# One order of 679 tasks for another in a sparse-attention and maxout kernel

## The chip, the cores and the metric

The kernel runs on one NeuronCore of a Trainium2 chip. The core has a matmul engine (PE; PEld is its weight load), three engines for elementwise work (DVE, ACT, POOL), and SP, which in this kernel does nothing but issue DMAs. Each engine works through its own list of instructions in order; semaphores make one wait for another. The metric is the device time of one execution, in microseconds, lower being better.

## The reference

Four batches, eight heads, 768 positions, head size 64. Each query sees the keys less than 16 positions away and, besides, 24 block summaries (the maximum of the keys and the mean of the values over blocks of 32). The result goes through a maxout layer.

```python
k_sum = k.reshape(B, H, nb, block, D).max(axis=3)
v_sum = v.reshape(B, H, nb, block, D).mean(axis=3)
scores_l = scale * q @ k.T        # kept where |i - j| < 16
scores_s = scale * q @ k_sum.T + log(32)
a = softmax(concat([scores_l, scores_s]))
x = a @ concat([v, v_sum])        # heads side by side: 3072 x 512
out = maximum(x @ w1, x @ w2) @ w_out
```

The kernel uses max(h1, h2) = h1 + relu(h2 - h1): it forms wd = w2 - w1, computes relu(x wd) w_out, and adds x (w1 w_out), with the product w1 w_out (called w1o) made once on the chip.

## The kernel before

The program is a list of 679 tasks. Each is made by `op` (L112) with the engines that may do it, a planned duration for each, what it reads and writes, and a label. `Plan.run` (L128) emits them in the sequence of the string `ORDER` (L20): each word has a letter for the engine (P, A, D, G for POOL, S for SP), the task's number, and the buffer slots that it takes. So `ORDER` fixes three things: the engine of each task, the sequence on each engine, and the slots. The planned durations are not read by `Plan.run`; of a table such as `{"SP": 1.3, "DVE": 1.0}` it looks only at which engines are named.

A task must wait for the tasks whose results it reads, for the former users of its slot, and for all that stands before it on its engine. The slots are few: 8 PSUM banks (most PE tasks take one or two), 8 landing buffers for loads (`land`), 4 for cast keys and queries (`kqb`), 1 for cast values (`vb`), 2 for spread values (`vx`), 4 for outputs (`o`).

The stages, with their lines, for batch b and head pair p:

- **Loads** (SP): keys and queries of a head pair, 384 KB each (`load_kq`, L305); values of half a batch, 768 KB (`load_v`, L327); the weights w1 and w2 in halves of 1 MB each (`load_w12`, L599) and w_out in two halves (`load_wo`, L629).
- **Keys and queries**: a cast to bf16 (L419), transposes on PE ("turn k", "turn q", L434), a copy out of PSUM ("place k", "place q", L453 and L465), for keys also the block maximum ("max", L454), a wrapped copy ("wrap", L458) and the summaries set into place ("sums", L461).
- **Values**: a cast (L331), five copies that spread them over tiles ("spread v", L371 to L377 and L387 to L393), block means on PE ("means", L346 or L349), their copies, and one copy that repeats them over all tiles ("spread means", L379 and L395). In batch 0 they are done in two halves of four heads. DVE, POOL, ACT (batch 0) or a DMA issued by SP can do a spread.
- **Attention**: "scores" (PE, L501), "exp" (ACT, L515), in batches 1 to 3 "mask" (DVE, L509), "values" (PE, L543), "inv" and "x" (DVE, L549 and L552), "turn x" (PE, L575) and its copy "xt". A score or value task carries two pairs of digits, head pair and group of 256 positions: "scores 0 01 11" is batch 0, pairs 0 and 1, group 1.
- **Weights**: "wd" (DVE or POOL, L607), "w1b" (cast, L610), "turn w1" (PE, L618), "w1t" (copy), "wo" (cast, L633), "w1o" (PE, L644: two half sums per quarter).
- **Maxout**, for each batch and group: four "hidden" tasks (PE, L660, eight matmuls of 256 columns), four "relu" (L666), then for each 128 rows "out" (PE): four matmuls with w1o (L674), twice four with w_out (L681), a copy (L685) and a store (SP, L692).

PE is used in four shapes: 128 rows by 128 columns (hidden, out, w1o, means of batch 0), 64 by 128 (all turns and the scores), 128 by 64 (values) and 128 by 32 (later means).

In the order before, the first loads are k02, k03, q02, k00, k01, q01, q00, v00, q03, v01, then the weights w1, w2 (first halves), w1 (second half), w_out (both halves), w2 (second half). The names k02 and so on are batch and head pair.

Of the kernel before, what the change touches and what calls it, by code (L numbers as in the profile page):

```python
# [17 lines left out]


ORDER = (  # L20
    "D3 S38:0,0 D6:0 S40:1,0 D1 D0 G7 D2 G4:0 S39:0 S12:2,0 S36:3,0 S37:0 G8 A92:0 S13:0 G5:0 A101:1 "
    "S14:4 P103:0,0 A93:2 P94:2,0 D105:3,0 G23:0,0,0 G9 A96:1,0 G32:0,0 S41:0 D68:3 D11:0 P70:4,0 S16:5 "
    "D97:0 P95:0 A77:1 D72:0,0 S42:6 P79:6,0 G78:0 D73:1 A81:2,0 G10 P80:0 D75 A100:0 D82:1 G69:3 D74 "
    "P71:0 D85:1 A76:2 S43:7 D83 D84 P88:2 D106:1 S52:0 P90:6 A89:0 D15:0,0 P86:4 A91:1 D19 P24:2 D102:2 "
    "D98 P104:0 D18 A25 S62:3 A20 D26 D22 A87:2 D17:0 S65:2 D108 A31 P33:3 D107 D21 A109:3 D27 D99 A34 "
    "D28 P114:6 A45:0 D29 P110:4 S53:4 D30 A115:3 P112:0 D35 P46:2 A111:4 G49:1 P116:6 D47:1,0 D117:0 "
    "A113:5 G48:0 S146:1,0 D118:0,0 P121:2 P126:4 D122:1 P50:6 D123:1,0 P119:0 D51:0 P124:2 A59:0 G44:0 "
    "D120:0 P131:6 S147:0 D125 A55:1 P60:0 D127:2 D128:0 P460:2 G63:0 A64:0 P56:3 D461:0 P458:5 S152:5,0 "
    "D57:0 A61:0 P455:2 D132:0 D133:0 P449:3 G66:0 A67:0 P136:0 P446:4 S150:6,0 D137:1 D138:0 P456 S153:0 "
    "P134:6 P450 D58:0 A135:1 S151:0 A457:0 P447 D54:0 S156:7 A451:0 P452:0 A448:0 S154:3 D218:1 P139:6 "  # L30
    "A219:0 P129:1 P453 D130 G257:3 A459 S149:2,0 D140:2 P220:3,0 P221:0 A454:0 G163:1,0,0,0 P480:1 "
    "D222:0,0 S148:0 A226:1 P141:6 P462:2 A481:1 D142:2 D223:1 A258:2 P482:5 G246:1 D143:0 A463 P464:0 "
    "D225 D224 D245:0 P144:3 S177:0,0 P227:6 A465 P476:1 D145 A228:2 D483 P484:2 A477 G157:0,0 P247:3,0 "
    "P248:0 P260:5,0 P259:0 D253:2 P471:0 A261:2,0 S172:4,0 D249:1,0 P478:7 A265:0 P472 D262:0 A479 "
    "P500:1 G155:0 D250:1 P489:3 A501:2 D229 A231:0 S161 P473 D263 S160 D264 G230:1 P164:4 S173:0 A474:0 "
    "P485 D168 S162 A165 D252 D159 P232:5,0 P266:0 P233:0 A234:3,0 P490 D166 D158 A167 P486 A238:3 S169 "
    "D235:0 S170:1,0 P491 A267:4 S171:0 D236 D237 P494:7 S180:5 D492:1 A487:2 P239:4 D251 S178:6 D495 "
    "P242:0 P269:2 A240:0 P496:6 D268 S174:7,0 A243:5 P498:7 D241 S475 P507:4 A497 D499 G294:2 A270:1 "
    "P272:0 P284:5 P502:7 D273:0 D244 A307:3 D271 P254:2 P503 A255:3 D274:2,0 S175:0 P508 D285:1 A295:1 "
    "D286:0,0 P275:0 D256 P287:2 P278:5 P509 G181:0,0 D288:2 D279:0 D289:0 P504 A510:3 D276:1 D280:0 "  # L40
    "S194:3,0 G306:0 P466:2 D277:0 P281:3 S488 P297:5,0 D282:2 P290:0 S176:0 A302:1 D283:0 P296:0 G179:0 "
    "P467 D291:3 A298:0,0 S493 P292:3 P468 G321:1 A505:0 D293 S186:0,0,0 G184 P188:5 D299:1 P309:0,0 "
    "S198:2,0 P308:0 P323:6,0 A314:3 P534:3 D310:3,0 S506 A469:2 P512:4 S182 D535:1 A325:2,0 S185 P518:0 "
    "D311:0 G187:0 G322:2 S470 P514:1 D333:3 A519:2 S196:1,0 D313 A513 P516:2 D312 D327 D326:0 G334:0 "
    "A515 P532:3 A517 G370:1 D189 D190 P335:0,0 S197:0 P336:0 D328 P324:0 A337:1,0 D533 P520:4 S183 "
    "A341:0 P530:2 D338:0 S199:0 A329:2 P521 D191 D339 S195:0 D300 A531 D340 P315:0 D192 P330:6 D193 "
    "P345:2 A316:2 P525:5 S204:5 A331:4 P522 D317 P536:0 A346:0 S200:4,0 D301 P543:1 D537 S202:6 P342:6 "
    "D332 P318:2 P544 A343:1 D347 S201:0 P552:0 A319:5 P303:6 D553:0 P545 G371:3 A304:3 P548:2 D320 "
    "A523:1 D344 S511 P526 A549 G382:0 D546:0 P354:6 P357:3 G397:2 P351:0 D355:0 P550:2 D356:1,0 D358:1 "
    "P527 D352:2 A551 D359:2,0 P554:6 D353:0 D305 P538:7 A555 A528:2 P373:2,0 P372:0 G383:3 P384:0,0 "  # L50
    "D378:2 P561:4 A374:2,0 G205:0,0 P348:5 A386:1,0 D375:0 P360:2 P562 D349:0 G203:0 P539 D350:0 D361:1 "
    "P563 D362:0 G410:1 S206:1,0,0 P363:5 A564:3 S529 P556:2 G409:0 D364:2 D365:0 S565 P366:3 D387:1 S208 "
    "P385:0 P368:5 A367:0 G398:3 P540 D369 G211:0 P557 A390:0 D377 D541:2 P570:3 D376 S542 D388 P558 D389 "
    "D571:2 P608:4 D209 A559:3 P411:5,0 S560 P394:0 D609:1 P379:2 P412:0 A395:5 S210 P579:7 D413:3,0 "
    "P572:4 A380:4 D417:3 P568:0 D207 A573 P400:5,0 P399:0 D414:0 P391:1 P590:3 A392:2 D401:0,0 P566:4 "
    "D416 D569 P588:1 A567 D403 D415 A591:0 P574:2 D393 A589 D402:1 P212:0 A405:1 P575 D213 A214 D215 "
    "P584:4 D381 D404 P576 D216 A585 D217 P406:5 P421:0 P580 A407:3 P592:3 D577:2 A422:1 P418:4 S578 P581 "
    "A419:0 D423 P586:6 D582:3 P604:2 S583 D587 S547 P602:0 D420 A605 D408 P593 A603 P439:4 P433:6 P424:1 "
    "P594 D425:0 D440:1 D441:0,0 P597:0 A595:2 D426:1,0 P606:4 S596 D434:2 D396 P598 A607 D435:0 P427:1 "
    "P436:3 P430:5 D428:1 P610:7 D437:0 D438:0 P599 D429:0 D431:2 P611 A600:3 D432:0 P615:3 S601 P442:1 "  # L60
    "P444:4 A443:3 P612 D445 P616 D613:0 P620:0 P674:6 P644:4 P660:5 D645:2 P658:1 P626:2 P622:7 A627:0 "
    "A621 P624:4 D623 P633:2 P642:0 P638:7 D643 P617 A639 A625 P646:0 D618:2 A661:1 P651:7 P634 P656:4 "
    "P640:3 A657 P664:5 D641 P662:4 P635 D663 P652 D659 A636:3 P647 S637 S619 P628:3 S524 P665 S614 "
    "P669:4 P629 P653 P666 A654:3 P630 S655 A667:2 P648 S668 D631:1 P675 S632 D649:0 P670 P676 S650 P671 "
    "A677:3 D672:2 S678 S673 "
)


# [34 lines left out]
class Plan:  # L103
# [8 lines left out]
    def op(self, engine, us, fn, read=(), write=(), change=(), touch=(), behind=(), prio=0.0, label="",  # L112
           port=False, lanes=(0, 1)):
        t = Task()
        t.port, t.lanes = port, lanes
        t.engine, t.us, t.fn, t.label = engine, us, fn, label
        t.on = us if isinstance(us, dict) else {engine: us}
        t.prio = (prio, len(self.tasks))
        t.new, t.behind = [*write, *change], behind
        t.deps = {w for b in (*read, *change) for w in b.writers}  # L120
        for b in t.new:
            b.writers.append(t)
        for b in (*read, *touch, *t.new):
            b.users.append(t)
        self.tasks.append(t)
        return t
# [20 lines left out]
def kernel(  # L147
# [15 lines left out]
    B, H, S, D = 4, 8, 768, 64  # L163
# [10 lines left out]
    op = plan.op  # L174
# [123 lines left out]
    def load_kq(b, hp, prio):  # L298
        f = Buf(land)
        for n, src in enumerate((k, q)):  # L300
            part = Buf(Ring([None]))
            view = lambda f=f, n=n: f.ap[:, 768 * n:768 * n + 768].rearrange("p (h c) -> p h c", h=2)
            kqin[b, hp, n] = f, part, view
            op("SP", {(0, 0, 0): 1.5, (0, 0, 1): 1.6, (0, 1, 0): 1.75}.get((b, hp, n), 1.09),
               lambda view=view, src=src: nc.sync.dma_start(  # L305
                out=view(), in_=src[b, 2 * hp:2 * hp + 2].rearrange("h (p j) d -> p h (j d)", j=J)),
               write=[f, part], prio=prio, label=f"load {'kq'[n]}{b}{hp}")

    v_spread, vx_part = {-1: []}, {}
# [73 lines left out]
    def later_values(b, prio):  # L383
        vb, parts = load_v(b, prio, 0, {"POOL": 1.52})
        kw = dict(write=[vx[b], *vx_part[b]], prio=prio + 2)
        last = []
        for piece, (lo, hi, tiles_, part, ms) in enumerate(PIECES):  # L387
            share = (1, 1, 1, 5 / 6, 1 / 6)[piece]
            last.append(copy({"SP": 0.05 + 2.15 * share * (hi - lo) / 64, "DVE": 0.1 + 0.87 * share,
                              "POOL": 0.1 + 2.9 * share},  # L390
                             lambda lo=lo, hi=hi, tiles_=tiles_, part=part, ms=ms: (
                                 rows(vx[b].ap[lo:hi, tiles_]), rows(vb.ap[part:part + hi - lo, ms])),
                             read=[vb], label=f"spread v{b}{piece}", **kw))  # L393
        mean = means(b, vb, [vb], 0, H, vx_part[b], prio + 2)
        v_spread[b] = [*last, copy({"SP": 2.1, "DVE": 1.9, "POOL": 5.7}, lambda: mean_rows(b, 0, H),  # L395
                                   read=[mean], label=f"spread means {b}", **kw)]

    def copy(us, aps, label, relu=False, **kw):
# [383 lines left out]
```

The softmax here doesn't subtract the row's maximum and nothing guards it: scores larger than these inputs give would overflow.

## Time and profile before

| | us |
|---|---|
| runs | 173.26, 173.74, 174.13, 174.36 (median 173.94) |
| the execution that was profiled | 174.36 |
| its span in the profile | 172.7 |
| PE busy | 154.5 |
| DVE busy | 113.4 |
| ACT busy | 89.2 |
| POOL busy | 40.3 |

The span begins 1.66 us short of the whole time of that execution. The granted clock of PE was 1.00 in every stretch. A row of the chain of waits gives a start, a length, and the engine and line that the end depended on; in a timeline, x is a count of instructions, and the bracket tells how long the engine stood idle before them and what released it. The duration of one instruction in a merged row is not the row's length divided by the count when instructions overlap.

### The profile page before, as it was taken

Reading aid. Unit: us, or ns where it says so; the run is one execution under the profiler, and the core shown is the slowest. Engines: PE = TensorE matmul, PEld = TensorE weight load, DVE = VectorE, ACT = ScalarE, POOL = GpSimd, SP = SyncE. Lnnn points to the kernel's source line nnn. Section 1 sums busy time; section 2 is a strip of 40 time slices with the busy share of each in tenths; the row PEclk is TensorE's granted clock in tenths of the full one; section 3 lists DMA queues with packets and bytes.
Section 4 is the critical chain, followed back from the end, with each engine's and each line's share of the span. In section 5 each row is a group of like instructions: output and inputs, shape, how many; then the busy total and the mean of one; then the engine's idle time right before and its main releaser. Section 6 shows DMA issues by size and latency. Waiting matters only on the chain.

```text
span 172.7 us, 5194 instructions
## 1 busy us (share of the span) xinstructions
PE 154.5 (89%) x2256; PEld 99.8 (58%) x2256; DVE 113.4 (66%) x208; ACT 89.2 (52%) x120; POOL 40.3 (23%) x61
## 2 busy tenths in 40 slices
PE   0257497999999999899999989999999999999992
PEld 0145266645865575468666645677565558856451
DVE  1399999555765978759998747799896741123031
ACT  2756787637765786347778251567553140231120
POOL 7540029322441001597001465200000000000000
PEclk9999999999999999999999999999999999999999
DMA  4999999999999299999999974720013110000645
GB/s 154 345 294 256 333 389 384 386 375 309 212 327 237 65 261 180 256 363 350 311 208 227 232 207 89 220 92 4 0 71 115 65 61 0 4 0 0 202 162 182
DMA packets 42742, 34.22 MB, mean 198 GB/s; under 512 B 25952, under 2 KB 36704, under 8 KB 42720
## 3 DMA queue, kind: packets, MB, share of 16 engines
q1 hardware_dynamic: 42720, 33.90, 69.2%
q8 instruction: 17, 0.28, 0.7%
q14 instruction: 5, 0.04, 0.1%
HBM read 25.17 MB, written 6.29 MB: 182 GB/s over the span
## 4 chain that ended last, share of the span: by engine, by line
PE 79%; SPq 9%; DMA 7%; ACT 2%; DVE 1%; issue 1%; DVEq 0%; ACTq 0%
PE banks L660 26%; PE banks L681 25%; PE banks L674 12%; DMA land<-in_moe_w_dram 7%; SPq L305 6%; PE banks L644 4%; PE banks L543 4%; PE banks L501 3%; PE banks L434 3%; SPq L599 3%; PE banks L575 2%; PE banks L346 1%; PE banks L618 1%; ACT w1b L410 1%; DVE qx L410 1%
## 5 line engine op out<-in xcount | busy, mean ns | idle before, releaser
L660 PE MATMUL banks<-xt,wd 128*128 128x256 bf16 x384 | 47.8, 277 | 0.0
L681 PE MATMUL banks<-wo,g 128*128 128x512 bf16 (+1 forms) x200 | 46.7, 371 | 0.0
L660 PEld LDWEIGHTS <-wd 128*128 128x128 bf16 x384 | 37.3, 99 | 9.0
L515 ACT ACTIVATE pb<-banks,bias 128x1024 bf16<-128x1024 f32 x24 | 25.8, 1113 | 7.7 <-PE banks L501 7.6
L406 ACT ACTIVATE g<-banks 128x512 bf16<-128x512 f32 x30 | 17.1, 601 | 22.1 <-PE banks L660 22.0
L681 PEld LDWEIGHTS <-g 128*128 128x128 bf16 x200 | 18.3, 98 | 17.0
L410 POOL CAST kqb<-land 128x768 bf16<-128x768 f32 x18 | 15.0, 849 | 43.5 <-DMA land<-in_k_dram 14.3
L674 PE MATMUL banks<-w1o,xt 128*128 128x512 bf16 (+1 forms) x100 | 24.7, 371 | 0.0
L408 DVE TENSOR_SCALAR g<-banks 128x512 bf16<-128x512 f32 x18 | 12.3, 689 | 15.2 <-PE banks L660 15.0
L410 ACT COPY o<-banks 128x512 f32<-128x512 f32 (+1 forms) x15 | 8.6, 571 | 24.1 <-PE banks L681 22.6
L434 PE MATMUL banks<-identity,kqb 64*128 64x64 bf16 x384 | 10.1, 202 | 10.1 <-POOL hide L242 6.3
L552 DVE TENSOR_TENSOR xs<-banks,inv 128x512 bf16<-128x512 f32 x24 | 16.1, 684 | 0.5
L434 PEld LDWEIGHTS <-kqb 64*128 64x128 bf16 x384 | 7.9, 102 | 13.6 <-ACT kqb L410 7.0
L454 DVE TENSOR_REDUCE ks<-kx 128x24 bf16<-128x768 bf16 x16 | 15.0, 943 | 1.1 <-ACT kx L410 0.9
L674 PEld LDWEIGHTS <-xt 128*128 128x128 bf16 x100 | 9.1, 98 | 7.9
L410 DVE COPY o<-banks 128x512 f32<-128x512 f32 (+1 forms) x10 | 6.6, 664 | 10.2 <-PE banks L681 8.3
L410 ACT COPY qx<-banks 128x768 bf16<-128x768 bf16 x12 | 9.5, 804 | 5.2 <-PE banks L434 2.3
L509 DVE TENSOR_TENSOR pb<-pb,mask 128x1024 bf16<-128x1024 bf16 x18 | 11.9, 680 | 0.3 <-ACT pb L515 0.2
L501 PEld LDWEIGHTS <-kx 64*128 64x128 bf16 x416 | 8.7, 102 | 5.3 <-issue 3.8
L543 PEld LDWEIGHTS <-pb 128*64 128x64 bf16 x384 | 8.2, 118 | 5.6 <-issue 4.0
L501 PE MATMUL banks<-qx,kx 64*128 64x64 bf16 (+2 forms) x416 | 10.3, 199 | 1.0 <-DVE kx L461 0.5
L410 DVE COPY kx<-banks 128x768 bf16<-128x768 bf16 x7 | 6.7, 952 | 6.7 <-PE banks L434 5.7
(63 smaller groups left out, 152.8 us busy)
## 6 DMA issues: line engine op xcount, KB each, us to landing
land<-in_k_dram SPq DMA_DIRECT2D x16, 384.0 KB, 6.9
land<-in_q_dram SPq DMA_DIRECT2D x16, 384.0 KB, 7.5
land<-in_v_dram SPq DMA_DIRECT2D x8, 768.0 KB, 10.3
out_dram<-o SPq DMA_DIRECT2D x19, 256.0 KB, 2.5
land<-in_moe_w_dram SPq DMA_DIRECT2D x4, 1024.0 KB, 11.1
land<-in_moe_w_out_dram SPq DMA_DIRECT2D x2, 1024.0 KB, 14.7
vx<-vb SPq DMA_DIRECT2D x3, 396.0 KB, 6.8
out_dram<-o SPq DMA_DIRECT2D x4, 224.0 KB, 3.4
```

The costliest lines, as they stand in the source:

```text
L406: nc.scalar.activation(out=o, in_=i, func=ACT.Relu)
L408: nc.vector.tensor_scalar_max(out=o, in0=i, scalar1=0.0)
L410: {"DVE": nc.vector.tensor_copy, "ACT": nc.scalar.copy, "POOL": nc.gpsimd.tensor_copy, "SP": nc.sync.dma_start}[e](out=o, in_=i)
L434: nc.tensor.transpose(out=bank(ps, 2048, BF16)[:, at:at + 64], in_=src.ap[r, j].rearrange("p h d -> p (h d)"), identity=identity[r, r])
L454: op("DVE", 0.95, lambda: nc.vector.tensor_reduce(out=ks.ap[:].rearrange("p (t s) -> p t s", s=2), in_=kt()[:, :, 0:64].rearrange("p t (s ...
L501: nc.tensor.matmul(**m)
L515: op("ACT", 1.13, lambda: nc.scalar.activation(out=pb.ap[:].rearrange("p a n -> p (a n)"), in_=bank(ps, 1024), func=ACT.Exp, bias=bias[:], ...
L543: nc.tensor.matmul(out=av()[64 * par:64 * par + 64, c, 2 * u + a, :], lhsT=pb.ap[:, a, at:at + 64], rhs=vx[b].ap[:, 4 * grp + 2 * u + par, ...
L552: op("DVE", 0.69, lambda: nc.vector.tensor_tensor(out=x.ap[:, grp] if g1 == grp else x.ap[:, grp:g1 + 1, hp % 2], in0=av()[:, :, :, 0:D], ...
L660: nc.tensor.matmul(out=bank(ps)[:, 256 * s:256 * s + 256], lhsT=wd[n].ap[:, c, 128 * s:128 * s + 128], rhs=x_rows(b, grp)[:, c, :], start= ...
L674: nc.tensor.matmul(out=bank(ps, hi - lo), lhsT=x_rows(b, grp)[:, c, sl], rhs=w1o[c].ap[:, lo:hi], start=(c == 0), stop=False)
L681: nc.tensor.matmul(out=bank(ps, hi - lo), lhsT=g.ap[:, f, sl], rhs=wo[f // 2].ap[:, f % 2, lo:hi], start=False, stop=(f == FC - 1))
```

## The change

`ORDER` is replaced as a whole, and the planned durations of three kinds of task are set to other values. The tasks, their code, the buffers and the arithmetic stay as they were.

```diff
 ORDER = (
-    "D3 S38:0,0 D6:0 S40:1,0 D1 D0 G7 D2 G4:0 S39:0 S12:2,0 S36:3,0 S37:0 G8 A92:0 S13:0 G5:0 A101:1 "
-    "S14:4 P103:0,0 A93:2 P94:2,0 D105:3,0 G23:0,0,0 G9 A96:1,0 G32:0,0 S41:0 D68:3 D11:0 P70:4,0 S16:5 "
...
-    "P444:4 A443:3 P612 D445 P616 D613:0 P620:0 P674:6 P644:4 P660:5 D645:2 P658:1 P626:2 P622:7 A627:0 "
...
+    "D2 G32:0,0,0 G5:0 D1 D0 D6:0 S36:0,0 D3 S12:1,0 S38:2,0 S40:3,0 G7 G4:0 S39:0 S13:0 A77:0 S37:0 G8 "
+    "P79:0,0 S41:0 D68:1 A81:2,0 P70:2,0 G92:2 S14:4 A72:1,0 P94:4,0 D101:3 S16:5 A96:0,0 D82:0 P103:6,0 "
...
+    "A672:3 S678 S673 "
 )
...
-            op("SP", {(0, 0, 0): 1.5, (0, 0, 1): 1.6, (0, 1, 0): 1.75}.get((b, hp, n), 1.09),
+            op("SP", 1.12,
...
-            last.append(copy({"SP": 0.05 + 2.15 * share * (hi - lo) / 64, "DVE": 0.1 + 0.87 * share,
+            last.append(copy({"SP": 0.05 + 2.8 * share * (hi - lo) / 64, "DVE": 0.1 + 0.87 * share,
...
-        v_spread[b] = [*last, copy({"SP": 2.1, "DVE": 1.9, "POOL": 5.7}, lambda: mean_rows(b, 0, H),
+        v_spread[b] = [*last, copy({"SP": 2.4, "DVE": 1.9, "POOL": 5.7}, lambda: mean_rows(b, 0, H),
```

Read back into labels, the two orders have these openings ("w" stands for w1 or w2, 0 or 1 for the half):

| | before | after |
|---|---|---|
| SP | k02 k03 q02 k00 k01 q01 q00 v00 q03 v01, w0 w0 w1 wo0 wo1 w1, k10 q10 k13 k12 q13 q12 v11 v10 q11 k11 | k01 k00 k02 k03 q02 q00 q01 q03 v00 v01, w0 w0 wo0 w1 wo1 w1, q10 q12 k10 q13 k13 k12 v11 v10 q11 k11 |
| ACT | casts k02 k03 q02, place k02, cast k01, place k01 q02 q00, exp 01 11, exp 02 12, means 00, spread v020, exp 00 10, spread v041, place q03, means 04, w1b 0, exp 22 32, 20 30, 21 31, w1b 3, w1b 2, wo 1 | cast k01, place k01 k00 k02 q00, cast q03, place q01 q03, exp 02 12, place q02, exp 01 11, spread v040, means 00, exp 00 10, spread v011, means 04, exp 20 30, 22 32, w1b 0, w1b 1, exp 21 31, w1t 1, wo 1, w1b 3 |
| POOL | amean, hide_t, amean, hide, ones 00, amean, ones 04, cast q01, ones, cast q00, w1b 1, wd 1, wd 0, wo 0, wo 2, cast k13 | ones 04, hide, amean, hide_t, amean, casts k02 q02 q00 q01, amean, ones 00, ones, spread v041, wd 1, wd 0, w1b 2, wo 3, cast k10 |
| DVE, from the cast of v01 on | cast v01, sums k03, wrap k03, spreads v030 v001, sums k02, spreads v011 v021 v031, spread means 01, w1t 0 | cast v01, spread means 00, spreads v001 v031 v021, spread means 01, inv 00 10, inv 01 11, x 00 10, inv 20 30, x 20 30, xt 000, w1t 0, xt 001 |
| PE, from the last early score task | scores 21 31, turn w1 0, values 00 10, 20 30, 01 11, turn w1 1, turn x000, x001, values 21 31, turn w1 3, hidden 001, turn w1 2, hidden 000, w1o 3, w1o 1 | scores 21 31, turn x000, turn w1 0, turn x001, turn w1 1, hidden 001, values 21 31, hidden 000, w1o 1, turn w1 3, turn w1 2, w1o 2, w1o 0 |

Over the whole order, DVE goes from 205 tasks to 201, ACT from 119 to 124, POOL from 41 to 42, SP from 82 to 80; PE keeps its 232. Of the spreads of batches 1 to 3, SP issued eleven before (v12, v13, v14, means 1; v20, v21, v23, v24; v30, v32, v34) and issues nine after (v12, means 1; v20, v22; v30, v31, v32, v33, means 3). In batch 2 POOL casts v21 before k20 in the new order (before: k20, then v21), and SP has the load of k21 between spread means 1 and the load of v21 (before: k20 and q20).

## The prediction

> **What bounds the kernel now.** The page first: busy shares, then the chain that ended last.
>
> ```profile
> PE 154.5 (89%) x2256; PEld 99.8 (58%) x2256; DVE 113.4 (66%) x208; ACT 89.2 (52%) x120; POOL 40.3 (23%) x61
> ...
> PE 79%; SPq 9%; DMA 7%; ACT 2%; DVE 1%; issue 1%; DVEq 0%; ACTq 0%
> ```
>
> PE carries four fifths of the chain. The remaining fifth lies almost wholly at the front, as the chain in order of time shows (start, length, what):
>
> ```profile
> 17.35 11.29 DMA land<-in_moe_w_dram
> ...
> 28.73 1.05 ACT w1b L410
> 29.79 0.05 issue
> 29.83 0.61 PE banks L618 x16
> 30.44 1.82 PE banks L660 x8
> 32.26 0.54 PE banks L618 x11
> 32.80 1.29 PE banks L660 x8
> 34.09 1.73 PE banks L644 x8
> ...
> 163.37 6.08 PE banks L681 x36
> 169.45 0.04 DVEq L410
> ```
>
> From 29.83 to 169.45 the chain is PE, but for two short detours, and then 3.25 us of copy and store to the end. So two things can move the time: when PE reaches its dense stretch, and what idles inside it. I take the end of "hidden 000" (34.09) as the mark, since both orders have nearly the same work behind it. The timeline of PE gives the idle behind it:
>
> ```profile
> 73.40 0.35 PE L434 MATMUL banks<-identity,kqb 64*128 64x64 bf16 x12 [0.58 <-ACT qx L410]
> ...
> 102.74 0.44 PE L543 MATMUL banks<-vx,pb 128*64 128x65 bf16 x16 [0.44 <-ACT kx L410]
> ```
>
> That is 0.58 + 0.44, with about 0.2 more hidden in modelled matmul ends: 1.2 us. What POOL does, and waits for, at the places that matter below:
>
> ```profile
> 26.01 4.67 POOL L607 TENSOR_TENSOR wd<-land,land 128x1024 bf16<-128x1024 f32 x2 [1.69 <-DMA land<-in_moe_w_dram]
> ...
> 40.34 0.83 POOL L410 CAST kqb<-land 128x768 bf16<-128x768 f32 x1 [4.92 <-PE banks L644]
> ...
> 43.67 0.83 POOL L410 CAST kqb<-land 128x768 bf16<-128x768 f32 x1 [2.33 <-DMA land<-in_q_dram]
> ...
> 70.09 1.48 POOL L410 CAST vb<-land 128x1536 bf16<-128x1536 f32 x1 [2.99 <-PE banks L681]
> ```
>
> **The planned durations** are no instructions: only the new order acts, so those edits cost nothing.
>
> **PE's own work behind the mark.** The new order leaves "turn w1 3" and "turn w1 2" behind the mark; before they lay ahead of it. Sixteen such matmuls in the dense stretch take 0.23 ("L501 x16" in the chain): +0.46. Against that, PE changes shape less often. In the chain an "out" of four matmuls takes 0.86 after its own kind and 0.97 after another shape: 0.1 per change. Counting along the two orders behind the mark, 68 changes become 65: -0.3. (In all 79 become 72; the rest lies in the front, under waits.) Net +0.16. The Trainium skill, "TensorEngine Tiling (Array Packing)", Key Properties, says that a change of tiling mode drains the engine and gives no price; taken alone it promises something from seven changes, the row says that at most three count.
>
> **The front.** SP issues the same bytes up to the weights, so what lands when follows from before: a waiting cast started at 4.39, 5.42, 6.57 for the first three loads and 9.07, 10.19, 11.32 for the fifth to seventh, 1.1 us per 384 KB. Now q03 is the eighth and v00 comes 1.1 later, v01 not later.
>
> - First turn: ACT casts k01 4.39 to 5.22, PE turns at 5.3 (before 6.31, as k03, the second load, was turned first). This buys nothing by itself, for the first scores need q01, the seventh load: 11.32, POOL cast 0.82, turn 12.2; but "place q01" now stands behind "cast q03" on ACT (eighth load, 12.45, cast to 13.3) and ends at 14.1. First scores end about 14.6, exp starts at 14.9; before it started at 14.95.
> - Values: cast v00 starts at 16.4 at the latest (15.36 before, plus 1.1) and ends at 17.35; four spreads on DVE at 0.57 bring 19.65, and cast v01 starts at 19.7, as before. Behind it DVE has 0.97 + 3 x 0.57 + 0.97 up to "spread means 01": done at 24.3, where before it was 25.75, because two summary copies and a wrap stand earlier, v030 too, and v011 went to ACT (1.51, beside it), while only spread means 00 came in.
> - Scores and exps: "means 04" on PE to 22.1, scores 20 30 and 22 32 to 23.5, exps of 1.06 on ACT from 22.95 to 25.1, then w1b 0 and w1b 1 (1.04 each, landed at 23.25) to 27.2, exp 21 31 to 28.3, w1t 1 to 29.3, wo 1 to 30.35. Before, POOL did w1b 1; that ACT now does both delays exp 21 31 by 0.9, covered by what follows.
> - "hidden 001" needs three things. xt 001: after 24.3 DVE has three inv and two x (2.05), xt 000, w1t 0, xt 001, ready at 27.95. Its predecessor on PE, turn w1 1, waits for w1t 0's bank and w1b 1: about 28.0. And wd 1: POOL, 26.01 + 2.35 = 28.36. So it starts at **28.4**, with 0.4 of cover. Before it was ready at about 29.5 and stood behind turn w1 3, which waited for the third weight load (28.7) and its cast. That wait is what the new order takes off the path.
> - It takes 1.82 (the row above), to 30.2; values 21 31 0.4; "hidden 000" waits for wd 0, 26.01 + 4.67 = 30.68, starts at 30.75 and takes 1.29: **32.05**, against 34.09.
>
> What is late next: w1o 1 needs wo 1 (30.35). turn w1 3 needs the second half of w1, now the fourth weight load instead of the third: one per 2.72 us after 26.0 gives 31.4, cast to 32.5, and PE asks at 32.9. The later half sums need wo 2 and wo 3 (34.2 + 1.05), asked for at 36.5. All covered, by 0.4 at the least.
>
> The Trainium skill, "TensorE: Matmul & The Clock Gate", The HAM clock gate, speaks against a full gain: PE runs at half rate until some 3.4 us of sustained work, in windows that do not follow the kernel. The rows agree in kind, at a granted clock of 1.00: the first hidden takes 1.82, the second 1.29, later ones 0.87. By the rows normal pace comes 2.5 us after the first hidden starts, and that carries over: 32.05. By the rule it comes at 31.8 or at the next window: 0.1 to 0.9 later. I take the row, since the new order presents PE with the same sequence here, and keep 0.9 for the range.
>
> **Sum.** Before, mark to end of PE 135.36, then 3.25. After: 32.05 + 135.36 + 0.16 + 3.25 = 170.8 against the span of 172.7, if the idle stays at 1.2: -1.9. The profiled execution (174.36) was 0.42 above the median of 173.94; the difference goes to the median: **172.0**. The last copy moves from DVE (0.42) to ACT (0.37), nothing.
>
> **The middle.** The two detours of before (bank waits behind ACT and DVE copies of the next batch) have other neighbours now. I costed the narrowest places with PE 2 us earlier. k10 is now the third load of batch 1: from 37.1 (last weight) to 43.67 six loads land, 1.1 each, so 40.35, POOL cast to 41.2, PE asks at 41.35. This also caps the gain: PE cannot be more than about 2 us early. On ACT, casts q22 and q23 with ten copies fill 75.6 to 83.65 without a hole, and "scores 2 20 21" asks for that bank at 83.7. Relu 022 frees a bank for scores 1 10 11 with 0.1 to spare, relu 123 one for turn k30. None costs by itself; each turns any lateness into idle PE. The nearest rows are the two detours, 0.4 to 0.75 each. Bounds: -1.2 (both go, none comes) to +2; I take zero net.
>
> **Spreads and DMA.** Three spreads leave SP for DVE and three for POOL; three from DVE and one from POOL go to it. The stretch 110 to 120 has DVE busy for 9.73 of 10 us and PE not idle, so a spread more on DVE is taken as hidden; without that cover one costs its 0.97. spread means 3 by DMA (4.1 us) is asked for at about 129, issued near 115.
>
> **Rivals.**
> *The gain is eaten by narrow places*: four of those above at 0.4 each, 1.6: 173.6, no change. For it: ACT's unbroken 8 us and the cap at k10. Against: before had as many narrow places and lost 1.2.
> *Slower, by values 2*: POOL now casts v21 ahead of k20 and k22. Before, spread means 1 was issued at 58.45, and the load of k20 behind it landed only at 66.27 and v21 at 70.05. If spread means 1 comes at 56.5 and only k21 lies between, v21 lands at about 67.5, k20 is cast by 70 and PE asks at 71.5: nothing lost. If v21 lands after 69.2, PE idles by the excess; at 72 its cast (1.48) and that of k20 (0.83) end at 74.3, 2.8 late at turn k20, and v20, landing 3.4 behind v21, makes means 2 another 0.5 late: 172.0 + 3.3 = 175.3. For it: DMA is full at 62 to 66. Against: fewer bytes stand before v21 than before.
> *More*: the two detours vanish and nothing comes: 170.8.
> That the text does nothing is excluded: `ORDER` is what is emitted.
>
> **Chances.** Forecast 0.52 (its own range 171.1 to 173.0), eaten 0.22, slower 0.20, more 0.06. A measurement tells 0.5% (0.87 us) from no change. Faster: 0.50 + 0.02 + 0.06 = 0.58; same 0.02 + 0.17 = 0.19; slower 0.03 + 0.20 = 0.23. Range 170.7 to 175.0: it leaves out half of "slower" and a part of "more".
>
> **What would show it.** POOL's two wd still near 26.0 to 30.7; the first hidden at 28.4; hidden 000 ended at 32.0; turn k10 at 41.3 to 41.5; PE idle behind the mark near 1.2; the last PE instruction near 167.6. Wrong, if the first weight pair lands later than 26.0, if hidden waits for xt or turn w1 1, or if PE idles at turn k20 or near 84.

## The result, and the profile after

| | before | after |
|---|---|---|
| median of all runs, us | 174.07 (56 runs, 172.65 to 175.9) | 173.6 (35 runs, 172.38 to 174.97) |
| ratio, with 95% interval | 1 | 0.9979 (0.996 to 0.9998) |
| the profiled execution | 174.36 | 172.48 |
| its span | 172.7 | 170.6 |
| end of hidden 000 (the mark) | 34.09 | 31.60 |
| from the mark to the end of the span | 138.6 | 139.0 |
| POOL begins the two wd | 26.01 | 25.83 |

The medians hold all runs, the ratios here and below only those within 1.5% of the fastest of their kernel, so that the two can differ a little.

The new order gains 0.5 us by the medians (0.2%), where the prediction had 1.9. Yet the two profiled executions differ by 1.88, and the span of 170.6 is within 0.2 of the 170.8 forecast. The profile agrees with the forecast and the runs don't; the work from here on was to find out why.

The page of the profile after, busy shares and shares of the chain:

```profile
PE 150.8 (88%) x2256; PEld 97.8 (57%) x2256; DVE 111.0 (65%) x204; ACT 92.0 (54%) x125; POOL 41.3 (24%) x62
...
PE 78%; SPq 9%; DMA 6%; issue 2%; DVE 2%; POOL 1%; ACT 1%; POOLq 0%
```

PE still carries the chain; POOL, 1%, is new in it. The chain that ended last, in order of time (start, length, what), shows where:

```profile
25.86 2.28 issue
28.14 2.37 POOL wd L607
30.51 0.04 issue
30.56 1.05 PE banks L660 x8
31.60 0.86 PE banks L644 x4
...
75.23 0.81 ACT qx L410
76.04 0.02 issue
76.06 0.96 DVE kx L410
77.02 0.86 DVE ks L454
77.88 0.88 DVE kx L410
78.76 0.04 issue
78.80 0.70 PE banks L434 x36
...
158.70 8.67 PE banks L681 x48
167.37 0.02 issue
167.39 0.37 ACT o L410
```

At the front the chain goes from the landing of the weights through POOL's two wd into hidden 000, as forecast. At 75 to 79 there is a detour that the order before did not have: PE waits at turn q22 for place k22 on DVE, which stands behind max k20 and place k21, and place k21 waits for place q21 on ACT, which reads the same pair of banks. The timeline of PE has both hidden tasks and the idle time:

```profile
29.05 1.05 PE L660 MATMUL banks<-xt,wd 128*128 128x256 bf16 x8
...
30.56 1.05 PE L660 MATMUL banks<-xt,wd 128*128 128x256 bf16 x8
...
72.44 0.35 PE L434 MATMUL banks<-identity,kqb 64*128 64x64 bf16 x12 [0.54 <-ACT kx L410]
...
78.80 0.70 PE L434 MATMUL banks<-identity,kqb 64*128 64x64 bf16 x36 [0.88 <-DVE kx L410]
```

Each hidden took 1.05, where the chain of before had 1.82 and 1.29. The same eight matmuls had taken 1.7 and 1.2 times as long there. Idle behind the mark is 0.54 + 0.88 = 1.42, against 0.58 + 0.44 = 1.02 before. The windows of PE (stretch, PE busy and count, granted clock as a share of the full clock, DMA share, GB/s) show a pace that changes within the front:

```profile
18.00:20.00 2.00, 0.00 (x0) 0.96 1.05 348
20.00:22.00 2.00, 0.71 (x4) 0.50 1.05 384
22.00:24.00 2.00, 2.00 (x30) 0.50 1.05 387
24.00:26.00 2.00, 2.00 (x74) 0.50 1.05 388
26.00:28.00 2.00, 1.50 (x52) 0.83 1.08 391
28.00:30.00 2.00, 1.44 (x32) 1.00 1.02 379
```

The clock was granted at half from 20 to 26 and was whole again by 28, just ahead of the hidden tasks.

### The profile page after: what moved, and what is told of

Its sections match the earlier page's. It is cut to its first block, busy times and chain, and to the rows that moved or that the text cites. A ratio compares the mean times of both kernels' runs of the same rounds, so it can differ in the third digit from the quotient of the medians.

```text
span 170.6 us, 5207 instructions
## 1 busy us (share of the span) xinstructions
PE 150.8 (88%) x2256; PEld 97.8 (57%) x2256; DVE 111.0 (65%) x204; ACT 92.0 (54%) x125; POOL 41.3 (24%) x62
## 4 chain that ended last, share of the span: by engine, by line
PE 78%; SPq 9%; DMA 6%; issue 2%; DVE 2%; POOL 1%; ACT 1%; POOLq 0%
PE banks L681 25%; PE banks L660 23%; PE banks L674 13%; DMA land<-in_moe_w_dram 6%; SPq L327 4%; PE banks L644 4%; PE banks L543 4%; PE banks L434 3%; PE banks L501 3%; SPq L305 2%; SPq L599 2%; PE banks L575 1%; POOL wd L607 1%; DVE kx L410 1%; PE banks L346 1%
## 5 line engine op out<-in xcount | busy, mean ns | idle before, releaser
L660 PE MATMUL banks<-xt,wd 128*128 128x256 bf16 x384 | 46.1, 273 | 0.1
L406 ACT ACTIVATE g<-banks 128x512 bf16<-128x512 f32 x25 | 14.9, 601 | 21.5 <-PE banks L660 21.1
L408 DVE TENSOR_SCALAR g<-banks 128x512 bf16<-128x512 f32 x23 | 15.5, 687 | 13.9 <-PE banks L660 13.6
L674 PE MATMUL banks<-w1o,xt 128*128 128x512 bf16 (+1 forms) x100 | 23.9, 371 | 0.0
L410 POOL CAST kqb<-land 128x768 bf16<-128x768 f32 x17 | 14.1, 837 | 35.0 <-DMA land<-in_q_dram 14.5
L509 DVE TENSOR_TENSOR pb<-pb,mask 128x1024 bf16<-128x1024 bf16 x18 | 12.8, 722 | 5.0 <-ACT pb L515 4.9
L410 ACT COPY qx<-banks 128x768 bf16<-128x768 bf16 x14 | 11.1, 800 | 4.1 <-PE banks L434 3.7
L410 POOL CAST vb<-land 128x1536 bf16<-128x1536 f32 x6 | 9.7, 1609 | 12.2 <-DMA land<-in_v_dram 12.2
L410 DVE COPY o<-banks 128x512 f32<-128x512 f32 x9 | 6.2, 690 | 8.9 <-PE banks L681 8.7
L410 ACT COPY kx<-banks 128x768 bf16<-128x768 bf16 x11 | 8.7, 802 | 5.4 <-PE banks L434 5.1
```

Source lines behind the costliest of these rows:

```text
L406: nc.scalar.activation(out=o, in_=i, func=ACT.Relu)
L408: nc.vector.tensor_scalar_max(out=o, in0=i, scalar1=0.0)
L410: {"DVE": nc.vector.tensor_copy, "ACT": nc.scalar.copy, "POOL": nc.gpsimd.tensor_copy, "SP": nc.sync.dma_start}[e](out=o, in_=i)
L509: nc.vector.tensor_tensor(out=o, in0=o, in1=m, op=ALU.mult)
L660: nc.tensor.matmul(out=bank(ps)[:, 256 * s:256 * s + 256], lhsT=wd[n].ap[:, c, 128 * s:128 * s + 128], rhs=x_rows(b, grp)[:, c, :], start= ...
L674: nc.tensor.matmul(out=bank(ps, hi - lo), lhsT=x_rows(b, grp)[:, c, sl], rhs=w1o[c].ap[:, lo:hi], start=(c == 0), stop=False)
```

## The experiments

### The same two kernels, profiled again

No edit: b_again and b_look are the kernel before, a_again and a_look the one after.

> The kernel before once more, for a second trace and more times. Clock theory (PE's pace in the front differs from execution to execution, and the profiled execution of before met a cold one): times spread over 172.7 to 175.9 as before; if this profile falls in the low half (under 173.5), its first hidden task takes about 1.05 and not 1.82 us and hidden 000 ends near 32.3 and not 34.1; if it falls in the high half, the trace repeats 1.82 and 34.1. Middle theory (the spread comes from waits behind the mark): hidden 000 ends near 34.1 whatever the time, and PE idle behind it differs from 1.2 us by what the time differs.

> The changed kernel once more. Clock theory: an execution near the median of 173.6 (span near 171.7) shows hidden 001 at 1.8 us and hidden 000 ending at 32.6 to 33, not 31.6, with the rest from the mark to the last PE instruction again at 135.8. Middle theory: hidden 000 ends near 31.6 again and the stretch behind it is 136.5 to 137.

> Before again, for a third trace. Clock and landing theory: the mark at span less 138.7. Middle theory: the mark at 34.1 to 34.5 and the stretch behind it differing from 138.7 by what the span differs from 172.7.

> The changed kernel again, for a third trace. Clock and landing theory (both traces so far were fast executions; a median one ends hidden 000 near 32.7, by a first hidden task at half pace or by a weight landing up to 1 us later, with 139.0 behind the mark): the mark lies at span less 139.0, whatever the span. Middle theory: the mark at 31.6 to 32.0 and more than 139.3 behind it when the span is over 171.5.

Medians: b_again 174.02 (ratio 0.9998, 0.9976 to 1.002), b_look 174.02 (1.0013, 0.9981 to 1.0045); a_again 173.33 (0.9969, 0.9945 to 0.9992), a_look 173.7 (1.0012, 0.9975 to 1.0048). In both profiles of before the first hidden took 1.82 or 1.80 again, in both of after 1.05. And again the profiled executions of before lay above their medians (174.96, 174.77) and those of after below theirs (173.02, 172.86). Three profiles of each kernel, set side by side, would have confirmed a gain of 1.9 that the runs do not show.

### Each order's front with the other's rest

```diff
-    (one order throughout)
+    (h_afterfront: tasks up to hidden 000 as in the order after, all others as in the order before)
+    (h_beforefront: the reverse)
```

> The changed order up to and with hidden 000, then all that is left in the sequence and on the engines of before (five slots moved). Front theory (the gain is made ahead of the mark, about 1.0 us in a median execution, and 0.3 to 0.4 is given back behind it): 173.1, faster than the changed kernel by 0.3. Rest theory (the 0.5 us come from fewer waits behind the mark, the front gives nothing because the clock and the landings take it): 174.0.

> The order of before up to and with hidden 000, then the rest as in the changed order. Front theory: 174.3 to 174.5, slower than before by 0.3. Rest theory: 173.5.

h_beforefront: 174.32, ratio 1.0012 (0.9986 to 1.0038), the idle at turn q22 present, hidden 001 at 1.82. It is no faster than before, so the rest of the new order shows no gain of its own. h_afterfront: 176.11, ratio 1.0126 (1.007 to 1.0182), and no answer: at the seam ACT had w1b 3 and w1b 2 one behind the other, and PE idled 0.62 and 0.54 ahead of turn w1 3 and turn w1 2. Slots had to be moved in it as well.

### Idle matmuls, first try

```diff
         make_identity(nc, identity[:])
+        for _ in range(HEAD):
+            nc.tensor.matmul(out=bank_tile[:, 0, 0:128], lhsT=identity[:], rhs=identity[:], start=True, stop=True)
...
         def mm():
+            for m in range(FILL if (b, h0) == (0, 4) else 0):
+                nc.tensor.matmul(out=bank(ps)[:, 0:4 * D], lhsT=amean[:, m % NM, :],
+                                 rhs=vb.ap[:, m % NM, 0:4, 0:D], start=True, stop=True)
             for m in range(NM):
```

HEAD and FILL are 36 and 14 in b_warm, 30 and 24 in a_warm.

> Before, with matmuls that nothing reads added in PE's idle times: 36 at the start, ahead of the first turn, and 14 in the gap before means 04. Clock theory: PE is at full pace by the first hidden task, hidden 000 ends near 32.3, and the time falls to 172.3 to 172.9, with less spread. Middle theory: no change, 174.0, or up to 0.5 slower by the added work.

> The changed order with the same added matmuls: 36 less 6 at the start, and 24 in the longer gap before means 04. Clock theory: hidden 000 ends at 31.6 (gated by wd 0 on POOL) in every execution, time 172.3 to 172.7; so against before with added matmuls the gain is 0.7 us or less, and the rest of the gain that was forecast was before's cold start. Middle theory: no change, 173.6, and the gain over the other is 0.5 as it was.

Both missed. a_warm, 174.69 (1.0028, 1.0007 to 1.005): PE ran at full pace where the matmuls were, from 16 to 26, and slowed down in the unfilled stretch behind them. hidden 001 started at 28.74, released by wd 1 as the prediction had it, but took 1.89, and hidden 000 1.82. b_warm, 178.95 (1.0268, 1.0225 to 1.0311), met something else; DVE's timeline:

```profile
24.57 3.86 DVE L418 COPY vx<-vb 64x1584 bf16<-64x1584 bf16 x3
28.46 2.87 DVE L418 COPY vx<-vx 32x2904 bf16<-32x2904 bf16 x1
```

In the profile of before the first group took 2.52 and the second 0.97. Here they fell beside POOL's two wd (25.66 to 30.50). The values came late, and hidden 001 with them (35.65).

### Everything 1 to 2 us later

```diff
         make_identity(nc, identity[:])
+        nc.vector.memset(land.slots[0][:, 0:LATE], 0.0)
```

LATE is 850 in a_late09 and b_late09, 1680 in a_late17 and b_late17. The first load waits for it, and all the rest behind.

> The changed kernel with one memset ahead of the first load, so that all that hangs on loads starts about 1.0 us later. Clock theory (the windows of the clock gate do not move with the kernel, so a shift changes which tasks of the front run at half pace, at random from one execution to the next): the median rises by 1.0, to 174.6, and the profiled execution can show hidden 001 at 1.8 us. Landing theory (the pace is fixed by the order, and the spread comes from when the loads land): every task keeps the duration that it had in the three traces of this order (hidden 1.05), median 174.6.

> The same with 1.9 us. Clock theory: median 175.5, and by now one of the two shifted traces shows half pace in the hidden tasks. Landing theory: median 175.5, durations as before.

> Before with the first load 1.0 us later. Clock theory: median 175.0, and the profiled execution can show hidden 001 at 1.05 us, where all three traces of this order had 1.82. Landing theory: 1.82 again, 175.0.

> Before with 1.9 us. Clock theory: median 175.9, one of the two shifted traces with hidden 001 at full pace and a mark that is then earlier by up to 1.5. Landing theory: 1.82 again, 175.9.

a_late09 174.44 (1.0018, 0.9988 to 1.0048), a_late17 175.14 (1.0062, 1.0032 to 1.0091), b_late09 176.35 (1.0113, 1.0016 to 1.0211, four runs), b_late17 176.38 (1.0129, 1.01 to 1.0159). At the larger shift the paces are exchanged: a_late17, order after, has hidden 001 at 1.89, and its profiled execution (176.47) is the longest of its runs; b_late17, order before, has both at 1.05, and its profiled one (175.17) is the second shortest. So the half pace does not belong to one order alone. The shift itself is no clean measure: b_late09 also had wd at 5.29 instead of 4.67.

### The idle time behind the mark, taken away

```diff
-D310:0,0 ... D299:0 ... D325:3,0      (place k21, max k20, place k22)
+D310:0,0 ... D325:3,0 D299:0          (a_fix1: max k20 last)
-P290:3 ... P297:0 ... P292:6          (turn x100, turn q20, turn x101)
+P290:3 ... P292:6 P297:0              (a_fix: this as well)
```

> The order after, with one task moved: on DVE, max k20 stands behind place k22 instead of ahead of it. Theory (the new stall at turn q22, 0.88 of idle PE in every profile of the order after, is a real cost): place k22 then ends near 77.9 on the profile's clock, as PE asks for its bank, the idle at turn q22 goes, and the stretch from the mark to the end falls from 139.0 to 138.2; the median is 0.7 to 0.9 below that of the order after (173.3 to 173.7 so far): 172.6 to 172.9, ratio to before 0.992 to 0.994. Rival (the idle only takes up a lateness that then shows at a later place, as scores 2 20 21): stall gone at turn q22, another one behind it, ratio 0.996 to 0.998.

> As the one before, and besides on PE turn q20 stands behind turn x101 instead of ahead of it, so that PE does not wait for place k20 (0.54 idle). Theory: both idles go, mark to end 137.7, median 172.1 to 172.5, ratio 0.989 to 0.991. Rival: 0.994 to 0.998, idle moved to a later place.

a_fix1 173.0 (0.9939, 0.9914 to 0.9965), a_fix 172.95 (0.9924, 0.9898 to 0.995). The first has the theory's ratio, and a median 0.1 above its figure. The second falls short of it by 0.45 us: its profile has both waits down, from 0.54 and 0.88 to 0.19 and 0.36, and its stretch from the mark is 138.35, but the median moved little against a_fix1. In a_fixd and a_hotfix below, which have both moves too, the stretch is 138.3, against 139.0 to 139.1 in the three profiles of after, so with both moves the wait was a real cost. a_fix1 alone shows it only in the median: in its profile PE still idles 0.67 at turn q22, with no cause shown. PE's timeline in a_fix (the release "issue" means a wait that the profile gives no cause for):

```profile
72.49 0.35 PE L434 MATMUL banks<-identity,kqb 64*128 64x64 bf16 x12 [0.19 <-ACT kx L410]
...
78.27 0.61 PE L434 MATMUL banks<-identity,kqb 64*128 64x64 bf16 x30 [0.36 <-issue]
```

The profile of a_fix1 brought two things that no other had. Its front is that of the order after, unshifted, and ran at half pace. PE's timeline:

```profile
27.83 1.89 PE L660 MATMUL banks<-xt,wd 128*128 128x256 bf16 x8
...
30.23 1.51 PE L660 MATMUL banks<-xt,wd 128*128 128x256 bf16 x8
...
65.44 0.67 PE L543 MATMUL banks<-vx,pb 128*64 128x65 bf16 x31 [1.44 <-DMA vx<-vx]
```

Its windows of PE, columns as above, say that the clock was taken back just there:

```profile
26.00:28.00 2.00, 1.13 (x41) 0.95 1.05 388
28.00:30.00 2.00, 2.00 (x20) 0.50 1.05 388
30.00:32.00 2.00, 2.00 (x22) 0.69 1.06 389
```

The last line of that timeline is the second thing: PE idled 1.44 at the values of batch 1 for the DMA of spread means 1. That execution took 174.43, the longest of its runs. The DMA issues (tile, queue, count, KB each, us from issue to landing) of before, in the stretch of that transfer:

```profile
vx<-vx SPq DMA_DIRECT2D x1, 363.0 KB, 4.1
```

and of a_fix1:

```profile
vx<-vx SPq DMA_DIRECT2D x1, 363.0 KB, 8.7
```

With the rest of before this transfer took 4.1 to 4.4 in all eight profiles. The order before issues it at 58.45, when the DMA engines have been 0.28 and 0.13 busy for 4 us. The order after issues it at 56.31 into a full queue (1.09 and 1.06), and it took 4.4 to 8.7 in the twelve profiles with that rest (5.7 in after's own). PE asks at 63.4 to 64.0; up to about 7 nothing is lost.

### Idle matmuls through the whole front

The edit of the first try, and besides, in the gaps (free columns of the same banks):

```diff
+    def idle(buf, tag):
+        for _ in range(IDLE.get(tag, 0)):
+            nc.tensor.matmul(out=bank(buf)[:, 256 + 8:512], lhsT=identity[:], rhs=amean[:, 0:2, 0:124],
+                             start=True, stop=True)
...
+IDLE = {'0 01 11': 4, '0 00 10': 3, 'x000': 3, 'x001': 3, 'w1 1': 7, '0 21 31': 4}
```

> The order after, with idle matmuls that keep PE busy: 30 at the start, 24 ahead of means 04, and 24 in the gaps between 22 and 30.5, into unused columns of the banks of values, turn x, turn w1. They change no output. Theory (the pace of PE in the front decides, and follows its load): both hidden run at 1.05 in the profile whatever the execution, hidden 001 near 28.8 after wd 1, hidden 000 near 30.7 after wd 0, mark 31.7; the median falls to that of the executions profiled so far (172.5 to 173.0), ratio 0.992 to 0.995, with a narrower spread. Rival (the pace of PE does not follow its load here, or the idle matmuls delay what stands behind them): hidden at 1.8 again, mark 33, ratio 1.000 to 1.006 as with the smaller filling.

> Both changes together: the idle matmuls and the two moved tasks. Theory: the sum, 171.2 to 171.8, ratio 0.984 to 0.987. Rival: as the better of the two alone.

a_hot 173.6 (0.9965, 0.9944 to 0.9987), a_hotfix 172.92 (0.9924, 0.9894 to 0.9954). The pace did what the theory said: in both profiles both hidden took 1.05, hidden 001 released by wd 1, hidden 000 by wd 0. The median did not: a_hot has the median of after, which was not timed beside it, and a_hotfix that of a_fix, which was. So no gain of full pace at the hidden tasks shows in the median of the order after. a_hot's profile has 0.44 of idle within the values of batch 1 that the profile gives no cause for, and its weights landed half a microsecond later than after's (wd from 26.35); whether the idle matmuls bring either is not settled.

### The engine of the last copy

```diff
-P671 A677:2 A672:3 S678 S673      (a_fix)
+P671 A677:2 D672:3 S678 S673      (a_fixd)
-A677:3 D672:2 S678 S673           (before)
+A677:3 A672:2 S678 S673           (b_enda)
```

> The order after with both tasks moved, and the last copy on DVE instead of ACT. In all runs so far the time outside the span is 1.70 in the median where the last copy is on DVE (before, and kernels that end as it does) and 1.82 to 1.90 where it is on ACT. Theory (the engine of the last copy makes that difference): 1.70 outside the span, the span 0.05 longer for the slower copy, median 172.7 to 172.9, ratio to before 0.991 to 0.9925. Rival (something else in the rest of the order makes it): 1.85 to 1.90 still.

> The order before with the last copy on ACT instead of DVE, nothing else. Theory: the time outside the span rises from 1.70 to about 1.88, the span falls by 0.05 to 0.1; ratio to before 1.000 to 1.001. Rival: 1.70 still, ratio 0.999 to 1.000.

a_fixd 172.9 (0.9897, 0.9858 to 0.9936), outside the span 1.70: as the theory had it. b_enda 174.56 (1.0026, 0.9983 to 1.007), outside the span 1.72: as the rival had it. The engine of the last copy alone does not make the difference; what does is open, and in the whole time neither edit shows. b_enda's profile gave more: the order before, not shifted, at full pace. PE's timeline:

```profile
30.64 1.05 PE L660 MATMUL banks<-xt,wd 128*128 128x256 bf16 x8
...
31.96 1.05 PE L660 MATMUL banks<-xt,wd 128*128 128x256 bf16 x8
33.43 1.89 PE L644 MATMUL banks<-wo,vx 128*128 128x512 bf16 x7 [0.42 <-POOL wo L410]
```

hidden 000 ends at 33.0 instead of 34.1, and that execution (173.82) lies below the median of its runs.

## Why the prediction was wrong, step by step

All profiles together take the front apart. The mark is set against the time at which POOL begins the two wd, which is the landing of the second weight load and varies by itself from 25.04 to 27.20 in the kernels that were not shifted:

| mark minus begin of wd, us | both hidden at 1.05 | hidden 001 at half pace |
|---|---|---|
| front of before | 6.66 (b_enda), 6.86 (b_late17) | 8.08 (before), 8.12 (b_look), 7.55 (b_again, h_beforefront) |
| front of after | 5.77 to 5.79 in nine profiles (after, a_again, a_look, h_afterfront, a_fix, a_fixd, a_late09, a_hot, a_hotfix) | 6.7 (a_fix1, a_warm), 7.07 (a_late17) |

b_late09 (half pace, 8.46) had slower wd and b_warm the collision on DVE; both are left out. Across a row the pace makes 0.7 to 1.5. Down a column the order makes 0.9 to 1.1 at full pace, 0.5 to 1.4 at half. The forecast difference was 34.09 - 32.05 = 2.04; the profiled one is 2.49. Both compare an execution of before at half pace with after at the normal one, or one partly so.

**Where the half pace comes from.** The windows of before read 1.00 while hidden 001 takes 1.82:

```profile
30.00:32.00 2.00, 2.00 (x24) 1.00 1.05 385
32.00:34.00 2.00, 2.00 (x27) 1.00 1.07 390
```

But the column counts a stretch for which the trace has no clock record as full, and the first record of before's trace begins at 33.39, inside hidden 000 (32.80 to 34.09, 1.29). So the 1.00 of its front, and with it the "1.00 in every stretch" ahead of the prediction, is no reading. The single matmuls of the hidden tasks and of the block means of batch 0 tell the pace. Up to 36 us in all twenty profiles, they start 0.165 to 0.214 apart where a record says 0.50 and likewise ahead of the first record, and 0.108 to 0.120 apart where a record says 1.00, without an exception. So in the three profiles of before, as in the others, hidden 001 at 1.8 to 1.9 lies under half a clock. The records last 3.41 us or a multiple of it, and begin at other times in each execution (16.44, 17.45 and 17.83 in the three of after). Cut into such stretches up to 45 us, the traces also show what goes ahead of a change:

| clock in a stretch of 3.41 us | in the next | stretches | PE busy in the first, us |
|---|---|---|---|
| half | half | 97 | up to 2.91 |
| half | full | 39 | 2.74 to 3.41 |
| full | half | 19 | up to 2.15 |
| full | full | 90 | 2.02 to 3.41 |

The last three stretches ahead of before's 33.39 had 2.83, 2.84 and 3.41. That puts the first two close to the change, and it shows why the place of the boundaries, which differs from one execution to the next, can decide the pace of a hidden task. It is a pattern of these twenty traces, read after the fact; no run was made to test it.

**The step that failed is the front's base**: "Before, mark to end of PE 135.36, then 3.25. After: 32.05", with its 34.09 as the mark of before. 34.09 was one execution's mark, not the kernel's. Unshifted, it is 33.0 at full pace (b_enda) and 33.4 to 34.7 with hidden 001 at half, and about half of the forecast gain was this difference. The prediction saw the matter: it set the rule of the Trainium skill ("TensorE: Matmul & The Clock Gate", The HAM clock gate: half rate until sustained work, in windows that do not follow the kernel) against the rows 1.82 and 1.29, and chose: "I take the row, since the new order presents PE with the same sequence here". The runs showed the reverse. With the same sequence hidden 001 took 1.05 or 1.8 to 1.9 under either order, and windows of the granted clock at 0.50 lay at 20 to 26 in after, 22 to 24 and 28 to 30 in a_fix1, 22 to 26 at 0.53 and 0.62 in b_enda. Here the rule was the better guide, and it had been used only to widen the range, and only for after. The "granted clock of 1.00" that it read beside its rows was the column without a record; by the first record full pace came at 33.39, 2.95 after the first hidden began, because a boundary lay there, and not as something that the order carries over.

**Correction of the median.** "The profiled execution (174.36) was 0.42 above the median; the difference goes to the median" was the only use made of that 0.42. It was a sign: the profiled execution was one of the longer kind. In the lists of runs the profiled executions at full pace mostly lie below their median (eight of eleven), those at half pace mostly above (six of eight; b_warm is left out). That fits a median between the paces. Of the other executions only span and mean clock are on record, and the mean, which counts missing records as full, doesn't tell where the clock was lost. Still, the time of before goes with it and that of after hardly does:

| mean clock of an execution | before: runs, median span | after: runs, median span |
|---|---|---|
| 0.996 to 1.00 | 122, 171.9 | 14, 171.5 |
| 0.99 | 50, 172.1 | 25, 171.8 |
| 0.98 | 86, 172.7 | 23, 171.3 |
| 0.97 | 5, 173.3 | 2, 172.3 |

(The runs of the two unedited kernels, over all sessions, that the ratios hold and that have a clock on record.) So the gain is no single number: in the spans it is 0.3 to 0.4 where little recorded clock is lost, and 1.4 at 0.98. Whether the new order meets full pace more often (in six of seven unshifted profiles without idle matmuls, against one of five with the front of before) stays open; a_hot speaks against much being left in it.

**Start of hidden 001**: forecast 28.4 (wd 1), measured 29.05. wd 1 was ready at about 28.2, as said. But the cast of v01, "at 19.7, as before", started at 20.27, when its load had landed, and the short tasks up to turn w1 1 ran at half pace (means 04 took 1.44; 0.82 in a_warm), so that turn w1 1 started at 28.71 instead of 28.0, and hidden 001 waited for it (to 29.05): one of the prediction's own signs of being wrong. In the profile this cost nothing, since hidden 000 waited for wd 0 anyway; at half pace it passes straight into the mark.

**hidden 000**: gated by wd 0, start 30.75 forecast, 30.56 measured. Right, and so firmly that nine profiles end it 5.77 to 5.79 after wd begins. That is 4.67 for the two wd, 1.05 for the task, and 0.05.

**Behind the mark**: "+0.16" for PE's own work and idle that "stays at 1.2". From mark to the end of the span it is 139.0 to 139.1 in after, a_again and a_look, 138.6 to 138.9 in before, b_again and b_look: +0.1 to +0.5 instead of +0.16. The new stall at turn q22 is in it, and the narrow places named (k10, scores 2 20 21, relu 022) are not: turn k10 came at 40.99 without idle, and nothing waits near 84. With one DVE task moved the median is 173.0 instead of 173.6, though the two were not timed side by side.

**Outside the span**: 1.70 with the order before in the median, 1.85 to 1.90 with the order after. The prediction had nothing there; +0.17, cause open.

The sum at equal pace: about -1.0 at the mark, +0.3 behind it, +0.17 outside, so -0.5, and the medians show -0.5. No term was fitted to that, but the three are known to some 0.2 each, and which paces the executions around the medians had is not known; so that they agree this closely is in part luck.

**Spread means 1** by DMA was in the rivals only as something for v21 to wait behind ("If spread means 1 comes at 56.5"; it came at 56.3). That the transfer itself, moved into a full queue, would take up to 8.7 and hold up the values was not seen. One profile of twelve shows the stall. How often it falls in the other runs is open; it can only make after's median worse than its profile.

**Values 2** did not hold anything up. The rival "eaten" gave the right time, 173.6, by the wrong places.

The version with both moved tasks is the fastest here: a_fix, ratio 0.9924 (0.9898 to 0.995) to before, where after has 0.9979, though it was not timed beside after; with the last copy on DVE, a_fixd, 0.9897 (0.9858 to 0.9936), which is not told apart from it.

## What to carry to other kernels

Before the gain of a change is read off one profiled execution, ask at which pace PE ran there and where that execution lies among its kernel's runs; one duration that differs between two identical tasks nearby (1.82 and 1.29 for hidden) is the sign. More profiles alone would not have done it: all three of before repeated 1.8. Where a clock column says 1.00, see whether the trace has a record there. Take the variable that comes from outside, here the landing of the weights, out of the comparison by measuring from it: the scatter of the marks of after's front then fell to 0.02 at equal pace. When an engine's wait goes, walk the new order for pairs of copies that read the same banks on two engines, and for transfers that are now issued into a full queue.

## What the runs showed of the hardware that was not expected

- The same eight matmuls took 1.05 or 1.80 to 1.89 in the front, in executions of one and the same order, and in all twenty profiles the clock records go with it; ahead of the first record (33.39 in before) the pace was the half one too, though the column reads 1.00.
- The clock changed at boundaries 3.41 us apart: from half to full only after a stretch with PE busy for 2.74 us or more, from full to half only after one with 2.15 or less.
- Idle matmuls kept PE at full pace only where they were: in a_warm the stretches up to 23.05 had PE busy for 2.9 to 3.0 us, the next (23.05 to 26.46) for 1.93, and from 26.46 the clock was at half (hidden 1.89); with the gaps filled (2.9 to 3.2 in each) it stayed full (a_hot, 1.05).
- DVE's copies from SBUF to SBUF were held up beside POOL's subtraction of the weights: 0.97 became 2.87, 2.52 became 3.86 (b_warm). The cast of wo on DVE ended 0.54 to 0.56 after the end of the second wd in all twelve profiles that have it there, whether it had begun 0.8 or 2.0 ahead of that end (1.55 long in after, 2.58 in a_hot), as if it could not run until wd was done. Copies out of the PSUM banks beside wd kept their 0.69 (28.20 in before, 27.97 in after).
- A transfer of 363 KB took 4.1 to 4.4 into a queue that had been nearly idle and 4.4 to 8.7 into a full one.
- ACT's and DVE's copies out of one pair of banks came one after the other: place k21 on DVE started at 76.06, 0.02 after place q21 on ACT had ended.
